# Another order for the last products, and other pieces of the last output rows

## The chip, the cores and the metric

The kernel runs on one core of one Trainium2 chip. A core has a matrix engine (TensorE, PE in the profile; its weight loads are PEld), a vector engine (VectorE, DVE), an activation engine (ScalarE, ACT), GpSimd (POOL), and SyncE (SP), which computes nothing and here issues DMAs. Sixteen DMA engines move data between the chip's memory (DRAM) and the core's on-chip memory; a DMA is issued from an engine's queue, here mostly SP's. Each engine runs its own list of instructions in order and waits on semaphores for the others. TensorE writes into PSUM, a small memory from which VectorE and ScalarE read.

The metric is the device time of one execution in microseconds (us); lower is better. Engine times within an execution come from a profile, which counts from the first instruction of the program to the last (the span).

## The reference

Attention with a block mask for 4 batches, 8 heads, 768 positions and 64 features a head; then a Fourier mixing over positions and features, a normalization, and two matrix products with a relu between them:

```python
attn = softmax(where(mask, scale * q @ k.T, -1e9)) @ v        # (4, 8, 768, 64)
x = attn.transpose(0, 2, 1, 3).reshape(4, 768, 512)
u = x + real(fft(fft(x, axis=1), axis=2))
un = (u - mean(u)) / sqrt(var(u) + 1e-6)
ch = maximum(un @ w_ch1, 0) @ w_ch2                           # 512 -> 2048 -> 512
return u + ch                                                 # (4, 768, 512) float32
```

## The kernel before

The work of a batch goes through attention, the Fourier stage, the normalization, the first product (`quad` in the kernel) and the second one. The program is one list of instructions in an order written out by hand: `slot` runs through the attention of all batches and puts pieces of the mixing of the batch before in between, by estimated times that `busy` adds up in `when`. After the last attention step only the last batch's mixing is left, and its pieces follow one another without anything between them. That last batch is done in another way than the first three (`last = b == B - 1`), and only it uses the functions `output_right`, `output_left` and `outputs`.

A batch's 768 rows stand in six tiles of 128 rows, three in `xA` (the first half, tiles 0 to 2) and three in `xB` (the second half, tiles 3 to 5). The Fourier stage wants rows s and -s together, so a tile's rows are not consecutive rows of the output. The table `_ORDER` says which they are: a tile is made of runs of rows, and `store` issues the DMAs for one tile: one for each run where the runs go backwards in the output, and one for a pair of runs where they go forwards. So tile 2 (`xA`, m = 2) leaves by two DMAs of 64 rows each, tile 5 (`xB`, m = 2) by one DMA whose rows are written as 2 x 64, and tile 4 (`xB`, m = 1) by one of 1 row, one of 2 x 63 rows, one of 1 row.

For the last batch the second product is done by Strassen's scheme in Winograd's form. The product has 2048 inner features; they are taken in two rounds (r = 0 and r = 1) of 1024. In a round, four `quad`s make the hidden features, then `outputs(r, m, after)` runs for m = 0, 1, 2. One call works on the pair of tiles m of `xA` and `xB` and splits each into its first 256 columns (a0 of `xA`, b0 of `xB`) and last 256 columns (a1, b1). Instead of eight block products it makes seven, named here by the order of Winograd's scheme: P1, P2, P3, P4 (right-hand sides 4), P5 (left sum 1), P6 (right-hand sides 2) and P7 (left sum 3). Each is four accumulating matmuls into one PSUM bank. VectorE then adds them into a0, a1, b0, b1 (`plus`), with a helper u that is P1 + P6 and later P1 + P6 + P7:

- a0 gets P1 + P2
- a1 gets P1 + P6 + P5 + P3
- b0 gets P1 + P6 + P7 + P4
- b1 gets P1 + P6 + P7 + P5

The left-hand sums of hidden features (`output_left(m, 1)` to `(m, 4)`) are VectorE work too. For m = 0 they are made inside the call; for the next tile they are made ahead, between this tile's sums (`ahead(j)`, which does nothing for the last m). The PSUM banks come from four pools: "m" and "s" of two banks, "t" and "o" of one. P1, P2, P3 use "m", P6 uses "t", P5 uses "o", P4 and P7 use "s". A bank can be written again once its reader has finished.

In the round r = 1 the finished rows are stored as each call goes on. In the last call (r = 1, m = 2, `ends` in the code) the second half's rows leave in three pieces: b1 once it is done, and b0, which is done last, in two DMAs of 128 columns, one from SP's queue and one from ScalarE's.

After the last store comes a branch: `with tc.If(over > 0): general()` (line 1574). `general` is a long slow path for inputs with very large scores; it is not taken here, but its code stands between the branch and the end of the program, and every engine has the branch in its list. Behind it each engine waits for what is outstanding, SP for the landing of all stores too, and a final barrier (line 1609) ends the program.

The lines that matter: 1115 to 1190 for the last batch's output stage, 1107 for the store, 1142 for the left-hand sums, 1159 for the matmuls of the seven products, 1166 for `plus`, 1175 for ScalarE's copy of P1, 1188 for the sum of u into both halves of `xB`, 1574 for the branch, 1609 for the end.

Of the kernel before, what the change touches and what calls it, by code (L numbers as in the profile page):

```python
# [82 lines left out]
def _rows(view, tile):  # L83

    got = []
    for t, p0, runs, jump, n, s0, step in _ORDER:
        if t != tile:
            continue
        at = view[s0:s0 + 1, :]
        row, col = list(at.ap[0])[0], list(at.ap[1])  # L90
        if jump > 0:
            got.append((p0, runs * n, bass.AP(tensor=at.tensor, offset=at.offset,
                                              ap=[[jump * row, runs], [step * row, n], col])))
            continue
        for r in range(runs):
            at = view[s0 + r * jump:s0 + r * jump + 1, :]
            got.append((p0 + r * n, n, bass.AP(tensor=at.tensor, offset=at.offset,
                                               ap=[[step * row, n], col])))
    return got
# [3 lines left out]
def kernel(  # L103
# [14 lines left out]
    nc = tc.nc  # L118

    B, H, S, D = q.shape  # L120
    DM = H * D
    FF = w_ch1.shape[1]
    P = 128
# [58 lines left out]
    ps_s = ctx.enter_context(tc.tile_pool(name="ps_s", bufs=2, space=PSUM))  # L182
    ps_o = ctx.enter_context(tc.tile_pool(name="ps_o", bufs=1, space=PSUM))
# [5 lines left out]
    when = {"PE": 0.0, "ACT": 0.0, "DVE": 0.0, "POOL": 0.0}  # L189
    free = {"m": [0.0, 0.0], "t": [0.0]}  # L190

    def busy(engine, us, after=0.0):
        when[engine] = max(when[engine], after) + us
        return when[engine]
# [283 lines left out]
    by_pe, to_gather = set(), deque()  # L478
    masks = {"by_pe": True}
# [68 lines left out]
    UP = 2 * C  # L548
    UNITS = len(pairs) * UP
    SLOT = 2  # L550
# [55 lines left out]
    def gather_to(u):  # L606
        while to_gather and to_gather[0] <= u:
            gather(to_gather.popleft())

    def gather(u):  # L610


        n, w = divmod(u, UP)
        half, c = divmod(w, C)
        if c == 0:
            return
        if c == 1:
            acc_of[n, half] = acc_p.tile([P, 2, HS], FP32, tag="acc", name="acc")
        acc, e = acc_of[n, half], e_of[u]
        start = e_of[u - 1] if c == 1 else acc  # L620
        at = max(e_at[u], acc_at.get((n, half), 0.0))
        if u in by_pe and masks["by_pe"] and w < UP - SLOT and max(when["DVE"], at) + 1.0 < max(when["POOL"], at) + 2.9:
            nc.vector.tensor_tensor(out=acc, in0=start, in1=e, op=ALU.add)
            acc_at[n, half] = busy("DVE", 1.0, at) + HOP
        else:

            for i in range(2):
                nc.gpsimd.tensor_add(out=acc[:, i, :], in0=start[:, i, :], in1=e[:, i, :])  # L628
            acc_at[n, half] = busy("POOL", 2.9, at) + HOP
        e_free[u] = acc_at[n, half]  # L630
# [320 lines left out]
    def mixer(b, xA, xB):  # L951
# [24 lines left out]
        t, s = {}, {}  # L976
# [127 lines left out]
        def store(half, m, cols=slice(0, DM), queue=nc.sync):  # L1104
            x = (xA, xB)[half]
            for p0, cnt, rows in _rows(out[b][:, cols], T * half + m):
                queue.dma_start(out=rows, in_=x[p0:p0 + cnt, m, cols])
            if m == T - 1:
                finished.add((b, half))
# [5 lines left out]
        o_t, o_s = {}, {}  # L1115
        DH = DM // 2

        def block(r, k, n):
            return w2_sb[:, 8 * r + 4 * k:8 * r + 4 * k + 4, n * DH:n * DH + DH]
# [10 lines left out]
        def output_left(m, j):  # L1130
            a11, a12, a21, a22 = (hs[g, i][:, :, m * P:(m + 1) * P]
                                  for i in range(2) for g in range(2))
            if j in (1, 3):
                o_s[m, j] = ep.tile([P, 4, P], FP32, tag="e", name="os")
            elif j == 4:
                o_s[m, j] = acc_p.tile([P, 4, P], FP32, tag="acc", name="os")

            to, a, c, op = {1: (o_s.get((m, 1)), a21, a22, ALU.add),
                            2: (a21, o_s[m, 1], a11, ALU.subtract),
                            3: (o_s.get((m, 3)), a22, a21, ALU.subtract),  # L1140
                            4: (o_s.get((m, 4)), a12, a21, ALU.subtract)}[j]
            tt(out=to, in0=a, in1=c, op=op)
            busy("DVE", 0.7)

        def outputs(r, m, after):

            if m == 0:
                output_left(m, 1)
                output_left(m, 2)
            a11, a12, a21, a22 = (hs[g, i][:, :, m * P:(m + 1) * P]  # L1150
                                  for i in range(2) for g in range(2))
            a0, a1 = xA[:, m, 0:DH], xA[:, m, DH:DM]
            b0, b1 = xB[:, m, 0:DH], xB[:, m, DH:DM]
            rights = {j: [o_t[j, 0], o_t[j, 1]] for j in (1, 2, 3, 4)}

            def product(pool, tag, a, c):
                ps = pool.tile([P, 512], FP32, tag=tag, name="yy")[:, 0:DH]
                for k in range(4):
                    nc.tensor.matmul(ps, a[:, k, :],  # L1159
                                     c[k // 2][:, k % 2, :] if isinstance(c, list) else c[:, k, :],  # L1160
                                     start=(k == 0), stop=(k == 3))
                busy("PE", 1.75)
                return ps

            def plus(to, a, c=None):
                tt(out=to, in0=a, in1=to if c is None else c, op=ALU.add)
                busy("DVE", 0.43)

            def ahead(j):
                if after is not None:  # L1170
                    output_left(after, j)

            u = sum_p.tile([P, DH], FP32, tag="oT", name="u")
            p1 = product(ps_m, "m", a11, block(r, 0, 0))
            nc.scalar.copy(out=u, in_=p1)
            plus(a0, p1)
            plus(a0, product(ps_m, "m", a12, block(r, 1, 0)))
            if m == 0:
                output_left(m, 3)
                output_left(m, 4)  # L1180
            plus(u, product(ps_t, "t", a21, rights[2]), u)
            plus(a1, u)
            p5 = product(ps_o, "o", o_s[m, 1], rights[1])
            plus(a1, p5)
            ahead(1)
            plus(u, product(ps_s, "s", o_s[m, 3], rights[3]), u)
            both = xB[:, m, :].rearrange("p (n d) -> p n d", n=2)
            tt(out=both, in0=both,
               in1=u.rearrange("p (o d) -> p o d", o=1).broadcast_to([P, 2, DH]), op=ALU.add)
            busy("DVE", 0.7)  # L1190
            plus(b1, p5)
            ends = r == 1 and after is None
            if ends:
                store(1, m, slice(DH, DM))
            ahead(2)
            p3 = product(ps_m, "m", o_s[m, 4], block(r, 1, 1))
            plus(a1, p3)
            if r == 1:
                store(0, m)
            ahead(3)  # L1200
            ahead(4)
            plus(b0, product(ps_s, "s", a22, rights[4]))
            if ends:
                store(1, m, slice(0, P))
                store(1, m, slice(P, DH), nc.scalar)
            elif r == 1:
                store(1, m)

        fl = [[("tm"[h == 1 and m != 1], lambda h=h, m=m: un_flip(h, m), 0.6, 0.55, 0.0)
               for m in range(T)]  # L1210
# [6 lines left out]
              for m, us in (((0, 2), RIGHT), ((1,), COMBINE))]  # L1217
        le = [("d", lambda i=i: left(0, i), 0.0, 0.0, COMBINE) for i in (1, 3, 4)]
        after = ([fl[0][0], sp[1][0]] + le +
                 [fl[0][2], sp[1][2], wh[1][0], fl[0][1], sp[1][1], wh[1][2],  # L1220
                  fl[1][0], fl[1][2], wh[1][1]] + ri[0] + [fl[1][1]] + ri[1])
        rest = []
        for r in range(2 if last else 0):
            rest += [(lambda p=p: quad(p), 7 * PRODUCT) for p in range(4 * r, 4 * r + 4)]
            rest += [(lambda r=r, m=m: outputs(r, m, m + 1 if m + 1 < T else None), 7 * 1.75)
                     for m in range(T)]
# [386 lines left out]
```

## Time and profile before

| what | value |
|---|---|
| median of 6 runs | 1064.7 us (1064.02 to 1069.03) |
| the profiled execution's own time | 1064.64 us |
| its span | 1062.9 us |
| mean granted TensorE clock | 0.997 |
| TensorE busy | 1036.2 us (97%) |
| the last batch's output stage, r = 0 | 942.5 to 979.1 us of the span |
| the same, r = 1 | 1015.2 to 1051.5 us |
| last sum on VectorE | 1051.54 to 1051.96 us |
| end of the span | 1062.9 us |

The span leaves out 1.7 us of the execution's own time. An idle engine costs nothing by itself; what counts is which engine, queue or transfer ended last, and in this program TensorE does until 1051.5 us. In the timeline, "x4" after a line is the number of instructions merged into it, and in square brackets stands how long the engine was idle before it and what released it.

### The profile page before, as it was taken

The page shows a single profiled execution, that of the slowest core. Times are in us where ns is not written, and L with a number is a line of the kernel's source. Part 1 is how long each engine was busy: PE and PEld are TensorE (multiplying, and loading weights), DVE is VectorE, ACT ScalarE, POOL GpSimd, SP SyncE. Part 2 cuts the span into 40 slices and gives each one's busy share as a digit, 9 for nine tenths or more (in the row PEclk, how much of TensorE's full clock was granted, in tenths as well). Part 3 has the DMA queues.
Part 4 walks back from the last instruction along what each step waited for, and adds up shares of the span by engine and source line. Part 5 has one row for each costly group of instructions (what it writes and reads, how often), then busy time and mean ns, then how long its engine had stood idle before and what let it go on. Part 6 is the DMA issues. An engine that isn't in the chain of part 4 may idle for free.

```text
span 1062.9 us, 12409 instructions
## 1 busy us (share of the span) xinstructions
PE 1036.2 (97%) x4390; PEld 536.2 (50%) x4390; DVE 654.0 (62%) x1218; ACT 374.1 (35%) x742; POOL 235.6 (22%) x262
## 2 busy tenths in 40 slices
PE   8999999999999999999999999999999999999995
PEld 4433345444455554444444555444445554578584
DVE  5899894667645445664578364765457355574663
ACT  6988855664030112342441302353221211210210
POOL 1000183537000002454553001256420001000000
PEclk9999999999999999999999999999999999999998
DMA  7757422220000002222230001221000001000001
GB/s 209 225 178 231 117 46 45 45 47 15 1 0 1 1 0 48 59 35 48 42 55 1 1 0 30 60 39 28 10 12 5 1 0 35 26 0 1 1 20 43
DMA packets 120741, 46.65 MB, mean 44 GB/s; under 512 B 108114, under 2 KB 113632, under 8 KB 120672
## 3 DMA queue, kind: packets, MB, share of 16 engines
q1 hardware_dynamic: 118654, 44.92, 17.1%
q10 hardware_dynamic: 1986, 0.85, 0.3%
q8 instruction: 36, 0.59, 0.2%
q14 instruction: 33, 0.27, 0.1%
q0 software_dynamic: 32, 0.01, 0.0%
HBM read 37.11 MB, written 6.29 MB: 41 GB/s over the span
## 4 chain that ended last, share of the span: by engine, by line
PE 87%; DVE 4%; ACT 3%; DMA 2%; issue 2%; SPq 1%; POOL 0%; ACTq 0%; POOLq 0%; DVEq 0%
PE y L1096 23%; PE z L1040 15%; PE s L569 11%; PE o L642 10%; PE yp L1040 7%; PE yy L1159 7%; PE xp L1040 4%; PE zp L850 2%; DMA out_dram<-x 1%; PE s L579 1%; PE zp L822 1%; PE sp L723 1%; PE utp L965 1%; ACT wraw L456 1%; ACT e L589 1%
## 5 line engine op out<-in xcount | busy, mean ns | idle before, releaser
L628 POOL TENSOR_TENSOR acc<-acc,e 128x384 f32<-128x384 f32 x158 | 159.3, 1044 | 94.1 <-DVE e L599 75.1
L569 PE MATMUL s<-qT,kT 64*128 64x384 f32 x768 | 153.2, 514 | 8.8 <-ACT e L589 5.3
L642 PE MATMUL o<-e,vr 128*64 128x384 f32 x768 | 141.7, 497 | 0.0
L1096 PE MATMUL y<-w_sb,hB 128*128 128x512 f32 x288 | 128.2, 596 | 1.0 <-DVE x L1099 1.0
L1096 PE MATMUL y<-w_sb,hA 128*128 128x512 f32 x288 | 128.4, 595 | 0.0
L599 DVE TENSOR_TENSOR e<-s,mask 128x768 f32<-128x768 f32 x92 | 83.8, 951 | 57.8 <-ACT s L597 48.0
L1099 DVE TENSOR_TENSOR x<-y,x 128x512 f32<-128x512 f32 x72 | 49.7, 690 | 110.9 <-PE y L1096 110.8
L569 PEld LDWEIGHTS s<-qT,kT 64*128 64x128 f32 x768 | 63.8, 185 | 87.1 <-issue 21.3
L597 ACT ACTIVATE s<-s 128x768 f32<-128x768 f32 x92 | 69.9, 792 | 87.6 <-PE s L569 87.0
L1040 PE MATMUL z<-unT,t 128*128 128x384 f32 x256 | 93.1, 486 | 1.2 <-DVE hA L1045 1.2
L628 POOL TENSOR_TENSOR acc<-e 128x384 f32<-128x384 f32 x42 | 47.1, 1142 | 212.3 <-ACT e L589 127.2
L1045 DVE TENSOR_TENSOR hA<-z,hA 128x384 f32<-128x384 f32 x64 | 35.7, 557 | 87.3 <-PE z L1040 87.3
L589 ACT ACTIVATE e<-s 128x768 f32<-128x768 f32 x100 | 76.1, 815 | 35.2 <-PE s L579 30.2
L1096 PEld LDWEIGHTS y<-w_sb,hB 128*128 128x128 f32 x288 | 53.4, 190 | 67.7 <-issue 64.8
L913 POOL TENSOR_SCALAR st<-st 128x1 f32<-128x1 f32 x24 | 8.6, 358 | 346.9 <-DVE st L912 346.9
L1096 PEld LDWEIGHTS y<-w_sb,hA 128*128 128x128 f32 x288 | 53.3, 190 | 62.8 <-issue 59.7
L642 PEld LDWEIGHTS o<-e,vr 128*64 128x64 f32 x768 | 47.9, 136 | 70.2 <-issue 68.3
L1049 ACT ACTIVATE hA<-hA 128x384 f32<-128x384 f32 x64 | 33.5, 523 | 120.3 <-DVE hA L1045 119.9
L1040 PEld LDWEIGHTS z<-unT,t 128*128 128x128 f32 x256 | 48.5, 190 | 35.5 <-DVE hA L1045 2.1
L1049 ACT ACTIVATE hB<-hB 128x384 f32<-128x384 f32 x64 | 33.5, 523 | 86.5 <-DVE hB L1045 84.2
L1060 ACT COPY hA<-xp 128x384 f32<-128x384 f32 x32 | 15.3, 478 | 97.9 <-PE xp L1040 97.9
L1040 PE MATMUL xp<-unT,w_sb 128*128 128x384 f32 x128 | 47.2, 492 | 0.0
(202 smaller groups left out, 1430.7 us busy)
## 6 DMA issues: line engine op xcount, KB each, us to landing
wraw<-in_moe_w_ch_dram SPq DMA_DIRECT2D x32, 512.0 KB
vr<-in_v_dram SPq DMA_DIRECT2D x30, 192.0 KB
qb<-in_q_dram SPq DMA_DIRECT2D x44, 96.0 KB
kb<-in_k_dram SPq DMA_DIRECT2D x44, 96.0 KB
x<-oT SPq DMA_DIRECT2D x192, 12.0 KB
out_dram<-x SPq DMA_DIRECT2D x17, 128.0 KB
out_dram<-x SPq DMA_DIRECT2D x7, 256.0 KB
qr<-in_q_dram SPq DMA_DIRECT2D x24, 64.0 KB
```

Of the source, the lines that this page charges most:

```text
L569: nc.tensor.matmul(s[:, i, 0:HS], kT[rows, c * P:(c + 1) * P], qT[rows, queries], start=True, stop=u not in by_pe)
L589: nc.scalar.activation(out=e, in_=s[:, :, 0:HS], func=ACT.Exp, scale=scale)
L597: nc.scalar.activation(out=s[:, :, 0:HS], in_=s[:, :, 0:HS], func=ACT.Exp, scale=scale)
L599: nc.vector.tensor_tensor(out=e, in0=s[:, :, 0:HS], in1=m.broadcast_to([P, 2, HS]), op=ALU.mult)
L628: nc.gpsimd.tensor_add(out=acc[:, i, :], in0=start[:, i, :], in1=e[:, i, :])
L642: nc.tensor.matmul(o[D * i:D * i + D, :], vt[:, i, c, :], e[:, i, :], start=(c == 0), stop=(c == C - 1))
L1040: nc.tensor.matmul(to, a[:, k, :], c[:, k, :], start=(k == 0), stop=(k == ND // 2 - 1))
L1045: tt(out=to, in0=ps, in1=a, op=ALU.add)
L1049: nc.scalar.activation(out=h, in_=h, func=ACT.Relu)
L1096: nc.tensor.matmul(y, hs[0, half][:, l, m * P:(m + 1) * P], w2_sb[:, 4 * r + l, :], start=(l == 0), stop=(l == 3))
L1099: nc.vector.tensor_tensor(out=x[:, m, :], in0=y, in1=x[:, m, :], op=ALU.add)
L1159: nc.tensor.matmul(ps, a[:, k, :], c[k // 2][:, k % 2, :] if isinstance(c, list) else c[:, k, :], start=(k == 0), stop=(k == 3))
```

## The change

In `outputs`, for every m and both rounds, P4 moves from the seventh place to the fourth, and P5 from the fourth to the sixth. The order P1, P2, P6, P5, P7, P3, P4 becomes P1, P2, P6, P4, P7, P5, P3. The sums move with them. The left-hand sums made ahead, which stood spread between the sums (1 after the sum of P5 into a1, 2 after the sums into `xB`, 3 and 4 after the sum of P3), now stand together: 1, 2 and 3 after the two sums of P5, ahead of the sum of P3, and 4 behind it.

In the round r = 1 the stores move as well. For m = 0 and 1 the second half's tile leaves after the sum of P5 into b1, the first half's after the sum of P3. For m = 2 the pieces are now: a0 after its second sum, b0 from ScalarE's queue after the sum of u into both halves, b1 after the sum of P5, and a1 at the end. Each is a half of the columns; the pieces of 128 columns are gone. The DMAs of that last call become 5 on SP's queue and 1 on ScalarE's, where there were 4 and 1.

In `gather` a comparison is given a name ahead of the `if` that uses it.

```diff
@@ gather
-        if u in by_pe and masks["by_pe"] and w < UP - SLOT and max(when["DVE"], at) + 1.0 < max(when["POOL"], at) + 2.9:
+        sooner = max(when["DVE"], at) + 1.0 < max(when["POOL"], at) + 2.9
+        if u in by_pe and masks["by_pe"] and w < UP - SLOT and sooner:
@@ outputs
+            ends = r == 1 and after is None
             u = sum_p.tile([P, DH], FP32, tag="oT", name="u")
             p1 = product(ps_m, "m", a11, block(r, 0, 0))
             nc.scalar.copy(out=u, in_=p1)
             plus(a0, p1)
             plus(a0, product(ps_m, "m", a12, block(r, 1, 0)))
+            if ends:
+                store(0, m, slice(0, DH))
             if m == 0:
                 output_left(m, 3)
                 output_left(m, 4)
             plus(u, product(ps_t, "t", a21, rights[2]), u)
             plus(a1, u)
-            p5 = product(ps_o, "o", o_s[m, 1], rights[1])
-            plus(a1, p5)
-            ahead(1)
+            plus(b0, product(ps_s, "s", a22, rights[4]))
             plus(u, product(ps_s, "s", o_s[m, 3], rights[3]), u)
             both = xB[:, m, :].rearrange("p (n d) -> p n d", n=2)
             tt(out=both, in0=both,
                in1=u.rearrange("p (o d) -> p o d", o=1).broadcast_to([P, 2, DH]), op=ALU.add)
             busy("DVE", 0.7)
+            if ends:
+                store(1, m, slice(0, DH), nc.scalar)
+            p5 = product(ps_o, "o", o_s[m, 1], rights[1])
             plus(b1, p5)
-            ends = r == 1 and after is None
-            if ends:
-                store(1, m, slice(DH, DM))
+            if r == 1:
+                store(1, m, slice(DH if ends else 0, DM))
+            plus(a1, p5)
+            ahead(1)
             ahead(2)
+            ahead(3)
             p3 = product(ps_m, "m", o_s[m, 4], block(r, 1, 1))
             plus(a1, p3)
             if r == 1:
-                store(0, m)
-            ahead(3)
+                store(0, m, slice(DH if ends else 0, DM))
             ahead(4)
-            plus(b0, product(ps_s, "s", a22, rights[4]))
-            if ends:
-                store(1, m, slice(0, P))
-                store(1, m, slice(P, DH), nc.scalar)
-            elif r == 1:
-                store(1, m)
```

## The prediction

> **What bounds the kernel now.** I read the chain that ended last first, then the stage that the diff touches, then what follows the last arithmetic. The chain in order of time ends so:
>
> ```profile
> 1015.24 36.27 PE yy L1159 x168
> 1051.51 0.02 issue
> 1051.54 0.42 DVE x L1166
> ```
>
> TensorE runs the 21 products of the last round without a gap: 36.27 / 21 = 1.727 us each. Then one sum, done at 1051.96. The span ends at 1062.9, so 10.9 us lie behind all arithmetic, and this chain does not explain them. Its waits do; from the branch's and the end's lines:
>
> ```profile
> L1574 PEldq COMPARE_BRANCH  x1: 3811/3811/3811, 1047.5 to 1047.5; - x1
> L1574 DVEq COMPARE_BRANCH  x1: 72/72/72, 1051.5 to 1051.5; - x1
> L1574 SPq COMPARE_BRANCH  x1: 50/50/50, 1052.6 to 1052.6; - x1
> L1574 ACTq COMPARE_BRANCH  x1: 62/62/62, 1053.4 to 1053.4; - x1
> L1574 DVEq EVENT_SEMAPHORE  x1: 21/21/21, 1056.1 to 1056.1; - x1
> ...
> L1574 ACTq EVENT_SEMAPHORE  x1: 17/17/17, 1060.9 to 1060.9; - x1
> ```
>
> Between its branch and its next instruction VectorE needs 4.5 us, though what that instruction waits for was over at 1052.0; TensorE's branch takes 3.8; ScalarE goes on 7.5 us after its branch, and SP's eight waits begin at 1060.9 too, 8.3 us after its own. From 1060.9 the closing waits and barrier take 2.0 us. So two things hold the end until 1060.9: stores that have not landed, and code that arrives late. The DMA view of the stretches behind (columns: stretch, its length, busy of PE, PEld, DVE, ACT, POOL, granted clock, DMA share, GB/s):
>
> ```profile
> 1027.60:1028.80 1.20, 1.20 (x7) 1.07 (x6) 0.39 (x2) 0.00 (x0) 0.00 (x0) 1.00 0.90 208
> 1041.70:1047.90 6.20, 6.20 (x31) 5.45 (x30) 2.00 (x5) 0.00 (x0) 0.00 (x0) 1.00 0.13 41
> 1050.90:1052.40 1.50, 0.60 (x3) 0.19 (x1) 0.42 (x1) 0.00 (x0) 0.00 (x0) 1.00 0.13 37
> ...
> 1055.90:1060.50 4.60, 0.00 (x0) 0.00 (x0) 0.00 (x0) 0.00 (x0) 0.00 (x0) 0.50 0.13 34
> ```
>
> The first is tile 0, two DMAs of 64 rows: 90% of the 16 DMA engines, 208 GB/s. The second is tile 4's 2 x 63 rows, the third b1's 2 x 64: share 0.13 is two engines of 16, at 37 to 41 GB/s. So `xB`'s tiles leave through two engines, `xA`'s through all. The last line is b0, issued at 1051.99 and moving only from 1055.9 to 1060.5, since its two engines still had b1 and their part of `xA`'s rows. In that stretch:
>
> ```profile
> q1 hardware_dynamic: 132, 0.07, 5.9%
> q10 hardware_dynamic: 130, 0.07, 4.9%
> q14 instruction: 3, 0.02, 1.9%
> ```
>
> SP's queue (q1) and ScalarE's (q10) move one piece of b0 each, and code (q14) comes in between.
>
> **The change part by part.** The sum is made against the profiled execution: 1064.64 us, span 1062.9, 1.74 around it; the median, 1064.7, stands 0.06 above it.
>
> *The comparison in `gather`, and the matmuls.* Same values, same matmuls: 0.
>
> *P4 fourth, P5 sixth.* P4 needs only hidden features and right-hand sides that were made in the quads. Each bank still has three or more products between uses, except P3's: it is last now, and the next tile's P2 takes its bank. The sum of P3 into a1 has the left-hand sums 1 to 3 ahead of it on VectorE. For m = 0, r = 1: P5 ends at 1015.24 + 6 x 1.727 = 1025.60; two sums start at 1025.63 and 1025.97 (neighbours start 0.34 apart now); left-hand sum 1 at 1026.31; 2 and 3, each waiting for the one before, 0.72 apart (0.68 long), at 1027.03 and 1027.75; the sum of P3 0.60 later, 1028.35 to 1028.77. The next P2 starts at 1027.33 + 1.73 = 1029.06, its first weight load 0.2 earlier: 0.1 to 0.3 us of room. Waiting behind that sum are left-hand sum 4 (until 1029.4) and a0's first sum, which follows ScalarE's copy at 1029.49 anyway. I take 0 for the four boundaries (two a round); bounds: 0, since TensorE has no gap to give back, and +0.8 (0.2 each, a load held until the sum ends).
>
> *Stores of m = 0 and 1.* `xB`'s tile leaves about 1.9 us earlier, `xA`'s about 2.3 later. The DMAs are the same and lie beside matmuls. What they can harm is the last tile: 2 x 63 rows took until 1048 on the two engines and end near 1046 now, before b0 asks for them. Below 0 is excluded, as nothing waits for them; above it by that slack. 0.
>
> *a0, two new issues on SP* at 1043.35 (P2 ends at 1042.88): 0.5 us of queue each, beside 8 us of matmul; nothing but b1's issue at 1050.3 is behind them. 0.
>
> *b0 earlier.* P7 ends at 1015.24 + 24.18 + 5 x 1.727 = 1048.06; its sum and the one into both halves end at 1049.23 (as now, 1048.54 + 0.69). ScalarE issues at 1049.25 and, at its 1.38 us, branches at 1050.65 instead of 1053.4. b1's issue at 1050.27 is 0.55 later than now.
>
> *The last issue.* P3 is done at 1051.51, the sum at 1051.96, as now. Then SP issues two DMAs instead of one, so it branches 0.57 later (0.52 long and a step), at 1053.16. ScalarE issues nothing there.
>
> *When the stores have landed.* b1 now moves 1.18 us after its issue (1049.72 to the 1050.9 of the third line). So b0 starts at 1050.45. b0 and b1 are 262 KB on two engines: at 51 GB/s (the steady part of tile 4's stretch, in finer slices) 5.1 us, at 37 GB/s 7.1 us, so until 1055.6 to 1057.5. Then a1's rows on these engines, 16 KB (0.4 us), and 0.4 us from the last packet (1060.5) to 1060.9: landed between 1056.4 and 1058.3 instead of 1060.9. All of b1 and most of b0 is moved while TensorE still works or in the 3 us after it.
>
> *When the code is there.* SP's own branch is the late one now. Bounds for what follows it: 3.8 us (TensorE's, few transfers beside it) and 8.3 (SP's now, which holds the landing too): 1057.0 to 1061.5. I take 5.0, near VectorE's 4.5, with 0.5 for a queue that is still busy around 1055: 1058.2. ScalarE, with 7.5 at the worst, is there at 1058.15.
>
> *The sum.* Both conditions met near 1058.3, less 2.6 from 1060.9. The closing 2.0 us stay. Span 1060.3, time 1060.3 + 1.74 = 1062.0.
>
> A rule that speaks against the change: the Trainium skill, "DMA: Bandwidth & Descriptors", in its section on where the fixed cost goes, fits a DMA as about 2.0 us plus bytes over 436 GB/s. By that the last store, issued at 1051.99, would have landed near 1054 now, and a second issue behind it would cost 0.57 us: 1065.2. The trace has 8.9 us for that store. The same page (section on why a DMA counts to 16) says that a DMA is spread over the largest number of engines up to 16 that divides its slowest dimension, lowest-numbered first, which is what the shares 0.90 and 0.13 show. "Runtime: NRT & Kernel Launch", on instruction fetch, says that a taken branch out of the loaded window fetches code by DMA before it goes on; the 4.5 us of VectorE agree.
>
> **The rivals.** Within 0.3% (3.2 us) of before is about what a measurement cannot tell from no change.
>
> *1. Code takes the place of the stores.* If ScalarE's and SP's 7.5 and 8.3 us are mostly code waiting behind whatever the two engines carry, SP's begins 0.57 later and lasts as long: ready at 1061.5, time 1065.2. For it: ScalarE owes nothing to a landing, yet goes on at 1060.9, when the stores end. Against: those engines empty some 3 us earlier then, and VectorE, branching in the same stretch, took 4.5.
>
> *2. The whole tail shrinks.* Code in 3.8 us, stores landed by 1057.0: span 1059.0, time 1060.7. For it: TensorE's branch. Against: b0 and b1 still lie on both engines when SP's code is asked for.
>
> *3. Slower: VectorE holds TensorE at the tile boundaries.* If P2's first matmul has to wait for the three left-hand sums put ahead of the sum of P3, 3 x 0.68 = 2.04 less the 0.27 of room is 1.8 us a boundary, 7.1 for four; less 2.6: 1069.1. It decides from (2.6 + 3.2) / 4 = 1.45 us a boundary. For it: room of 0.1 to 0.3. Against: the order above is worked from starts that the profile shows.
>
> **How the numbers follow.** Forecast 0.55, its own range 1061.0 to 1063.3; rival 1, 0.20; rival 2, 0.18; rival 3, 0.07. The likeliest gives 1062.0. Faster by over 0.3% is under 1061.5: rival 2 and about 0.12 of the forecast, 0.30. Slower by over 0.3% is rival 3, 0.07. The same holds 0.63. The range reaches to rival 2's side, 1060.2, and to most of rival 1, 1064.9, which leaves out its upper part and rival 3.
>
> **What would show it.** TensorE's last matmul at 1051.5 within 0.3 us and no gap over 0.2 at a tile's second product (else rival 3). ScalarE's branch near 1050.7, SP's near 1053.2. The last packets of q1 between 1056.2 and 1058, none of q10 after. SP's closing waits starting at 1057.5 to 1059. If q1 and q10 are empty by 1057 and SP's waits still begin at 1060.9 or later, rival 1 is right, and my prediction is wrong in its step on the code.

## The result, and the profile after

The changed kernel takes 1062.67 us (median of 19 runs, 1061.76 to 1063.69) where the kernel before takes 1064.83 (42 runs). The ratio is 0.9978, with a 95% interval of 0.9972 to 0.9984: 2.2 us, or 0.22%, less. That is under the 0.3% within which the prediction calls two kernels the same, but the interval lies clear of 1, so the kernel did become faster. The profiled execution took 1062.0 us, its span is 1060.3.

The chain of the changed kernel ends as it did before, with the 21 products of the last round:

```profile
1008.28 3.87 PE z L1041 x12
1014.73 36.36 PE yy L1160 x168
```

They take 36.36 us where they took 36.27, and this execution came to them 0.5 us earlier, in code that the change does not touch. So all times below are counted from the end of the last matmul, which is 1051.08 us of the span after and 1051.50 before. From there to the end of the span it was 11.43 us and is 9.21: the 2.2 us that the medians show lie there.

The branch's lines after (an engine's branch, and the first waits behind it):

```profile
L1576 SPq EVENT_SEMAPHORE  x8: 17/17/17, 1057.5 to 1058.6; - x8
...
L1576 ACTq COMPARE_BRANCH  x1: 62/62/62, 1050.0 to 1050.0; - x1
...
L1576 DVEq COMPARE_BRANCH  x1: 72/72/72, 1051.1 to 1051.1; - x1
L1576 SPq COMPARE_BRANCH  x1: 50/50/50, 1052.8 to 1052.8; - x1
L1576 DVEq EVENT_SEMAPHORE  x1: 21/21/21, 1054.0 to 1054.0; - x1
L1576 ACTq EVENT_SEMAPHORE  x1: 17/17/17, 1055.5 to 1055.5; - x1
```

ScalarE branches at 1050.0 and goes on at 1055.5, 5.5 us later, long before the end; VectorE needs 2.9 us. Neither is near the end any more. SP's first wait passes at 1057.46, and the trace has b1's landing at 1057.45; its second and third pass at 1057.89 and 1058.24, where the trace has the two pieces of a1 landing on the last DMA engine at 1057.87 and 1058.23. So SP had its code by then, and waited for rows.

What moved between (first the DMA queues from 1050.1 to 1053.9, then from 1053.9 to 1057.4; columns: packets, MB, share of 16 engines):

```profile
q10 hardware_dynamic: 129, 0.13, 12.4%
q1 hardware_dynamic: 16, 0.02, 3.8%
q8 instruction: 1, 0.02, 1.5%
q14 instruction: 1, 0.01, 0.7%
...
q1 hardware_dynamic: 274, 0.25, 24.9%
q14 instruction: 5, 0.04, 3.2%
q10 hardware_dynamic: 1, 0.00, 0.0%
```

In the first stretch nearly all is b0, from ScalarE's queue (q10): 0.13 MB, on the two DMA engines that 12.4% of sixteen are. b1 had been issued from SP at 1049.84, but no packet of SP's queue moves before 1053.3. In the second stretch come b1 and a1 (q1), and five code blocks between them.

### The profile page after: what moved, and what is told of

Same layout as the page of the kernel before. It is cut to its first block, busy times and chain, and to the rows that moved or that the text cites. A ratio compares the mean times of both kernels' runs of the same rounds, so it can differ in the third digit from the quotient of the medians.

```text
span 1060.3 us, 12418 instructions
## 1 busy us (share of the span) xinstructions
PE 1037.0 (98%) x4390; PEld 535.7 (51%) x4390; DVE 654.6 (62%) x1218; ACT 374.5 (35%) x742; POOL 235.7 (22%) x262
## 4 chain that ended last, share of the span: by engine, by line
PE 89%; DVE 3%; ACT 2%; DMA 2%; issue 1%; SPq 1%; POOL 0%; ACTq 0%; DVEq 0%
PE y L1097 23%; PE z L1041 15%; PE s L569 12%; PE o L643 11%; PE yp L1041 7%; PE yy L1160 7%; PE xp L1041 4%; PE zp L851 2%; PE s L579 1%; PE sp L710 1%; DMA out_dram<-x 1%; PE zp L823 1%; PE sp L724 1%; PE utp L966 1%; PE xt L666 1%
```

## The experiments

Theory 1, at the start: the second half's rows go through two DMA engines, which empty them one piece after the other, and the landing of the last of them holds the end. Theory 2: code that ScalarE and SP fetch behind the branch comes late and holds the end, and the change helps because ScalarE branches earlier.

All times below are medians, each beside runs of the kernel before on the same chip (1065.09 in the runs 1 to 4, 1064.3 in 5 to 8, 1064.43 in 9 to 12). The lines of the kernels differ by a few from those of the profile before.

### 1 and 2: no branch

```diff
-    with tc.If(over > 0):
-        general()
```

> The kernel before without the branch and the slow path behind it (the slow path, which these inputs never take, is left out). Theory 1, the last rows on two DMA engines hold the end: the stores stay where they are, only the code blocks no longer come between them, so the end of the span moves by at most 1.5 us, to 1063.3 or more of 1064.8. Theory 2, code that ScalarE and SP fetch late holds the end: 3.5 to 5 us faster, 1059.8 to 1061.3.

> The changed kernel without the branch and the slow path. Theory 1: the last landing (1058.2 of the span now) still holds the end, at most 1 us faster than the changed kernel, 1061.7 or more. Theory 2: its code is what is left, so it loses 2 us or more, to 1060.7 or less, and stands close to the kernel before without the branch.

The kernel before without the branch: 1063.62 us, ratio 0.9983 (0.9974 to 0.9992), 1.5 us faster. The changed kernel without it: 1060.92, ratio 0.9955 (0.9942 to 0.9969), 4.2 us faster than before and so about 1.8 faster than with the branch. Theory 2 wanted 3.5 to 5 us in the first, and the two kernels close together: they stand 2.7 us apart. The first fits theory 1 (1.5 us was its bound). The second lies between the two: theory 1 had allowed 1 us, theory 2 had asked for 2, and it gave 1.8 (its 1060.92 is 0.8 us below theory 1's bound and 0.2 above theory 2's).

The traces split what the branch costs. Counted from the last matmul, the last rows land at 8.39 us instead of 9.38 in the kernel before, at 5.87 instead of 7.15 in the changed one: 1.0 and 1.3 us of transfer. And from the last landing to the end of the span it is 1.4 and 1.25 us instead of 2.05; SP's eight waits behind the branch, which take about 0.6 us when nothing stops them, are gone. That second part I had not counted. So code does cost, but not by being late: its blocks get in the way of the rows. The trace names no DMA engine, but it shows this twice. In the kernel before, a code block moves from 1059.36 to 1059.66 and no row moves in that time, though 31 rows of b0 are still to come. And in the changed kernel the last piece of a1 lands on its two late engines at 5.95 and 7.15 us, without the branch at 5.85 and 5.87: with the code one of the two falls behind.

### 3: ScalarE's piece issued from SP

```diff
-                store(1, m, slice(P, DH), nc.scalar)
+                store(1, m, slice(P, DH))
```

> The kernel before, with the second 128-column piece of b0 issued from SP's queue too. ScalarE then branches some 10 us earlier and its code is there long before the stores have landed; the rows, their order and their two DMA engines are the same, SP branches 0.6 us later. Theory 1: 1064.8 within 0.6. Theory 2 (ScalarE's late code): 2 us or more faster, 1062.8 or less.

1063.82 us, ratio 0.9984 (0.9975 to 0.9993), 1.3 us faster. Neither: more than theory 1's 0.6, less than theory 2's 2. The branch's lines of this kernel:

```profile
L1574 SPq EVENT_SEMAPHORE  x8: 17/17/17, 1058.8 to 1060.6; - x8
...
L1574 ACTq COMPARE_BRANCH  x1: 54/54/54, 1041.5 to 1041.5; - x1
L1574 ACTq EVENT_SEMAPHORE  x1: 17/17/17, 1046.6 to 1046.6; - x1
...
L1574 SPq COMPARE_BRANCH  x1: 50/50/50, 1054.1 to 1054.1; - x1
```

ScalarE is through with its code at 1046.6, before the last tile's rows begin, and the end is still held: the last rows land 8.29 us behind the last matmul instead of 9.38, at 1060.2, and the rest of SP's waits pass behind that. The gain is 1.1 us of landing, nearly the same as without the branch. Theory 2 as stated falls here. What stays of it becomes part of theory 1: code blocks that are fetched while the last rows move delay them, by about 1 us in all. This run also puts both pieces of b0 into one queue; that this is not what helped follows from runs 2 and 10 (below).

### 4 and 9: the second half's rows later

The fourth run stored b0 (ScalarE) and b1 (SP) behind a1; the ninth issued both from SP:

```diff
-            if ends:
-                store(1, m, slice(0, DH), nc.scalar)
...
-            if r == 1:
-                store(1, m, slice(DH if ends else 0, DM))
+            if r == 1 and not ends:
+                store(1, m)
...
                 store(0, m, slice(DH if ends else 0, DM))
+            if ends:
+                store(1, m, slice(0, DH), nc.scalar)        # run 9: without nc.scalar
+                store(1, m, slice(DH, DM))
```

> The changed kernel, with b0 and b1 of the last call stored behind a1, at the end. Products, sums, pieces and queues are the same; only the time at which the two engines' rows leave is moved, b0 by 2.7 us, b1 by 2.2. Theory 1: the landing moves by as much, 1064.5 to 1065.5, the gain is gone. If the order of the products is what brings the gain: 1062.7 within 0.5.

> The changed kernel, with b0 and b1 of the last call both issued from SP, behind a1. In the run before this one only b1 was late: ScalarE's queue waits for nothing but b0's own sum, so it had issued b0 when it always does. Now b0 leaves 4.0 us later than in the changed kernel, b1 3.6. Theory 1 (two DMA engines empty the second half's rows one piece after the other, and that holds the end): they start 2.9 us after the last matmul and need 6 to 6.5 us, the end moves by 2 to 3 us, 1064.4 to 1065.7. If the order of the products or the cut into halves is what brings the gain: 1062.7 within 0.5.

Run 4: 1062.34 us, ratio 0.9971 (0.996 to 0.9982), as fast as the changed kernel. The expectation was wrong, since its premise was: ScalarE's queue waits for nothing but b0's sum, so b0 was issued 2.23 us ahead of the last matmul's end, exactly as in the changed kernel, and only b1 was late, by 3 us. That this cost nothing is a finding of its own: in the changed kernel b1's first row moves 2.3 us behind the last matmul, when b0 is nearly through (its last rows end at 2.5 and 2.8), so b1 gains nothing by being issued sooner.

Run 9 does what run 4 was meant to do, with the order of products, the halves and all sums as in the changed kernel: 1064.8 us, ratio 1.0001 (0.9992 to 1.001). The whole gain is gone. Its lines:

```profile
L1577 SPq EVENT_SEMAPHORE  x8: 17/17/17, 1057.5 to 1061.3; - x8
...
L1577 ACTq EVENT_SEMAPHORE  x1: 17/17/17, 1046.8 to 1046.8; - x1
...
L1577 DVEq EVENT_SEMAPHORE  x1: 21/21/21, 1054.4 to 1054.4; - x1
L1577 SPq COMPARE_BRANCH  x1: 50/50/50, 1054.5 to 1054.5; - x1
```

SP's waits begin 3.0 us after its branch, so its code is early, and they last until 1061.3: b1 lands at 1061.0, 9.65 us behind the last matmul. Its closest neighbour is run 10 (below), which also issues everything from SP and differs only in the place of the two stores: there b0 leaves 4.2 us sooner and b1 3.8, the last landing is 3.8 us sooner, and the median, 1061.33, is 3.5 us lower. The order of the products is worth nothing by itself; it is worth what it does for the time at which the second half's rows leave.

### 5 and 11: whole tiles, and pieces without the new order

```diff
 # run 5, on the changed kernel
-            ends = r == 1 and after is None
+            ends = False
 # run 11, on the kernel before
+            if ends:                      # behind the second sum of a0
+                store(0, m, slice(0, DH))
...
-                store(0, m)
+                store(0, m, slice(DH if ends else 0, DM))
...
-                store(1, m, slice(0, P))
-                store(1, m, slice(P, DH), nc.scalar)
+                store(1, m, slice(0, DH), nc.scalar)
```

> The changed kernel, with the last call's tiles stored whole like the others: xB's after the sum of P5, xA's after the sum of P3 (no halves, no issue on ScalarE). Theory 1: the two engines start on 262 KB 1 us later than they do now, and carry 8 rows of 2 KB of xA behind it instead of 1 KB: landing 1 to 1.7 us later, 1063.7 to 1064.4. If the halves are worth nothing: 1062.7 within 0.3.

> The kernel before with its own order of products, but the new pieces: a0 leaves after its second sum, b1 after the sum of P5, a1 after the sum of P3, b0 last as one piece from ScalarE. Theory 1: b0 still comes last on the two engines, which only have 4 rows of 2 KB less to move in front of it: 0.3 to 1 us faster than before, 1063.6 to 1064.3 where before is 1064.6. If the cut into halves is the gain: 1062.5.

Run 5, the new order with whole tiles: 1062.65 us, ratio 0.9983 (0.9974 to 0.9992). The last landing is at 7.50 us behind the last matmul, 0.35 later than in the changed kernel, not the 1 to 1.7 of the expectation. But this run changes two things, for without b0's own issue ScalarE is out of the tail: it branches at 1042.2. The run that shares this and keeps the halves is again run 10, and beside it whole tiles land 1.7 us later (7.50 and 5.82), as expected, with ratios 1.3 us apart (0.9983 and 0.9971). So the halves do seem to be worth something, and what ScalarE's code costs hides it in the comparison with the changed kernel. The intervals of these two ratios overlap a little, so by the times alone it is not shown.

Run 11, the pieces with the old order: 1063.03 us, ratio 0.9986 (0.9977 to 0.9995), 1.4 us faster, more than the 0.3 to 1 expected. a0 leaves early, b0 leaves in one piece of 1 KB rows, and the last landing is at 7.92 us instead of 9.38. So the pieces alone bring more than half of what the whole change brings. The gains of the parts do not simply add up, since all of them relieve the same two engines, and what the new order brings with ScalarE left in the tail and whole tiles was not run.

### 6: no b0 at all

```diff
             if ends:
-                store(1, m, slice(0, P))
-                store(1, m, slice(P, DH), nc.scalar)
+                finished.add((b, 1))
```

> The kernel before without the store of b0 (those rows' first columns are left out of the output). It measures what the last store costs by itself. Theory 1: the end falls to the landing of xA's rows (1057.2 of the span) or SP's code, 3 to 4 us faster, 1060.8 to 1061.8. Theory 2: SP and ScalarE branch 0.6 and 10 us earlier, and SP's code still takes 8 us: 1064.2.

1059.54 us, ratio 0.995 (0.9937 to 0.9964), 4.8 us faster than before. That is the price of the kernel before's last store, and more than expected; it includes what ScalarE's code costs, since without an issue of its own ScalarE branches at 1042.4. The lines show what is left without it:

```profile
L1573 SPq EVENT_SEMAPHORE  x8: 17/17/17, 1056.9 to 1057.4; - x8
...
L1573 DVEq COMPARE_BRANCH  x1: 72/72/72, 1052.7 to 1052.7; - x1
L1573 SPq COMPARE_BRANCH  x1: 50/50/50, 1052.8 to 1052.8; - x1
L1573 DVEq EVENT_SEMAPHORE  x1: 21/21/21, 1057.2 to 1057.2; - x1
```

SP's eight waits all pass within 0.5 us, and begin 4.1 us after its branch; the last rows had landed 0.2 us before that. VectorE needs 4.5 us. So here the rows are no longer what SP waits for; what comes last is most likely its code, 4.1 us behind the branch in this run.

### 7, 8, 10 and 12: what the theory says would be better

Run 7 moves P2 of the last call behind P5, so that b0 and b1 are done one product earlier. Run 8 issues b1 from GpSimd's queue. Run 10 issues b0 from SP's queue. Run 12 is run 7 with b0 from SP's queue.

```diff
 # runs 7 and 12, on the changed kernel
-            plus(a0, product(ps_m, "m", a12, block(r, 1, 0)))
-            if ends:
-                store(0, m, slice(0, DH))
+            if not ends:
+                plus(a0, product(ps_m, "m", a12, block(r, 1, 0)))
...
             ahead(3)
+            if ends:
+                plus(a0, product(ps_m, "m", a12, block(r, 1, 0)))
+                store(0, m, slice(0, DH))
 # runs 10 and 12
-                store(1, m, slice(0, DH), nc.scalar)
+                store(1, m, slice(0, DH))
 # run 8: store(1, m, ..., nc.gpsimd) for b1
```

> The changed kernel, with P2 moved behind P5 in the last call alone: P1, P6, P4, P7, P5, P2, P3. b0 and b1 are done and leave one product (1.73 us) earlier, a0 two products later. Theory 1: the two engines are empty 1.7 us earlier, and a1's part follows without a wait; the end falls by 1 to 1.7 us to 1061.0 to 1061.7, unless SP's code now comes last. Theory 2: SP's branch is where it was, 1062.7 within 0.3.

> The changed kernel, with b1 issued from GpSimd's queue instead of SP's. If its rows go to other DMA engines than b0's, theory 1 says that the two queues empty side by side and the end falls by 1 to 2 us, 1060.7 to 1061.7; if they go to the same two engines, 1062.7 within 0.5. GpSimd's own work for the DMA can cost as much as is gained, since it starts only after b1's sum.

> The changed kernel, with b0 issued from SP's queue in the same place. The rows leave when they do now; ScalarE has nothing at the end and branches 8 us earlier, so its code blocks come before the rows. Theory 1: the two engines lose no time to ScalarE's code, 0 to 1 us faster, 1061.7 to 1062.7. If ScalarE's issue beside SP's is worth something: slower than 1062.7 by 0.3 or more.

> The version with P2 behind P5 in the last call (second half's sums first), with b0 issued from SP's queue, so that ScalarE's code is loaded long before the end. Theory 1: the end falls by 0 to 1 us below that version's 1060.8, to 1059.8 to 1060.8; the bound below is SP's code, 4.1 us after its branch in the run without b0, which gives 1060.0.

| run | median, us | ratio to before | last landing | end of the span |
|---|---|---|---|---|
| before | 1064.83 | 1 | 9.38 | 11.43 |
| changed | 1062.67 | 0.9978 (0.9972 to 0.9984) | 7.15 | 9.21 |
| 7 | 1060.83 | 0.9966 (0.9954 to 0.9978) | 6.05 | 7.93 |
| 8 | 1062.62 | 0.9981 (0.9972 to 0.999) | 7.19 | 9.02 |
| 10 | 1061.33 | 0.9971 (0.996 to 0.9981) | 5.82 | 7.88 |
| 12 | 1059.67 | 0.9956 (0.9942 to 0.9969) | 4.46 | 6.43 |

(Landing and end in us behind the last matmul, from one profiled execution each.) Run 10's profiled execution took 1063.75 us, 2.4 above that run's median, but it lost this ahead of its last matmul. Run 7 was faster than expected by 0.2 us, run 10 by 0.4, run 12 by 0.1; the kernel before was 0.4 to 0.5 us faster beside these runs too, so they came out about as expected. Taken one by one, 7 and 10 touch or overlap the changed kernel's interval; run 12 does not, and is the fastest version here: 4.8 us under the kernel before and, by the two ratios, some 2.3 under the changed one.

Run 10 and run 2 belong together. With b0 on SP's queue and ScalarE's code out of the way the last landing is at 5.82; with b0 on ScalarE's queue and no code at all it is at 5.87. So the queue by itself costs nothing, and the 1.3 us to the changed kernel's 7.15 are put down to ScalarE's code (each landing is from one execution). From run 7 to run 12 the same move is worth 1.6 us of landing. The lines of run 10:

```profile
L1576 SPq EVENT_SEMAPHORE  x8: 17/17/17, 1059.6 to 1060.3; - x8
...
L1576 ACTq EVENT_SEMAPHORE  x1: 17/17/17, 1049.7 to 1049.7; - x1
...
L1576 SPq COMPARE_BRANCH  x1: 50/50/50, 1056.4 to 1056.4; - x1
```

Run 8 brought nothing. GpSimd needed 0.95 us to issue the DMA, its rows began only 2.4 us behind the last matmul, when b0 was nearly through, and b1 was now the last to land, at 7.19, where from SP's queue it had landed at 6.37 with a1 behind it. The trace does not name the DMA engines, but the rows of b1 move at most two packets at a time, and two of the sixteen shares of a1 land late (5.8 to 6.8 us, the others by 4.5) as they do in the changed kernel; so b1 again went through two engines only, and through two that a1 needs as well.

In run 12 the waits behind the branch look like those without b0:

```profile
L1578 SPq EVENT_SEMAPHORE  x8: 17/17/17, 1055.1 to 1055.7; - x8
...
L1578 ACTq EVENT_SEMAPHORE  x1: 17/17/17, 1046.3 to 1046.3; - x1
...
L1578 SPq COMPARE_BRANCH  x1: 50/50/50, 1052.4 to 1052.4; - x1
L1578 DVEq EVENT_SEMAPHORE  x1: 21/21/21, 1054.7 to 1054.7; - x1
```

SP's waits begin 2.7 us after its branch and pass without a stop: nothing is left that waits for rows alone. The bound of 1060.0 in the expectation, worked from the 4.1 us of run 6, did not hold: how long the code takes differs from run to run.

### The runs together

From the last landing to the end of the span it is 1.7 to 2.1 us in every run that has the branch and all stores, from the fastest (4.46 and 6.43) to the slowest (9.65 and 11.51), and the medians follow. In the run without b0, where code most likely comes last, it is 2.25. This is what shows theory 1: as long as SP's code is there first, the last landing sets the end, and it moves with the time at which the two engines get their rows and with what else they carry, the code among it.

## Why the prediction was right

The forecast was 1062.0, the result 1062.67; the size was 2.7 us forecast, 2.2 measured. By its steps:

- *P4 fourth, P5 sixth: 0, bounds 0 and +0.8.* The weight load of the next tile's P2 did wait for the sum of P3: 0.18 us at each of two boundaries in the last round, and 0.7 us of VectorE waits in all for the four. TensorE's stage became 0.09 us longer, 36.36 for 36.27; the first round 0.08. So the term is +0.2. Rival 3 is excluded by these numbers. The lines for one boundary:

```profile
1027.85 0.42 DVE L1167 TENSOR_TENSOR x<-yy,x 128x256 f32<-128x256 f32 x1
1028.18 0.68 DVE L1143 TENSOR_TENSOR os<-hA,hB 128x512 f32<-128x512 f32 x1
1028.32 1.59 PEld L1160 LDWEIGHTS yy<-w_sb,hA 128*128 128x128 f32 x8 [0.18 <-DVE x L1167]
```

  The sum of P3 ends at 1028.27, and the weight load starts behind it. On the clock of the profile before that is 1028.78, as forecast (1028.77); but the load was due before it, so the 0.1 to 0.3 us of room were not there, and it was the bound that covered the loss.
- *Stores of m = 0 and 1, and a0: 0.* No later piece waited for them. Right.
- *b0 earlier.* Forecast 2.26 us ahead of the last matmul's end, measured 2.23; ScalarE's branch 0.86 ahead, measured 1.08 (its issue took 1.13 us, not 1.38). Right.
- *The last issue.* SP's branch 1.65 us behind the last matmul, measured 1.72. Right. a1's second issue took 0.65 us.
- *Landing between 1056.4 and 1058.3.* On the same clock, 4.9 to 6.8 us behind the last matmul; measured 7.15. This is the term that was mis-sized, by 0.4 us beyond its upper end: of what the two engines lose to code blocks I had counted nothing, and runs 1 to 3 put that at 1.0 to 1.3 us. The prediction also had all of b1 and most of b0 moved within 3 us of the last matmul. It was the other way round: b0 was through by then and b1 had only begun, since b1 waits for b0. That changes nothing in the sum, which takes both together.
- *Code, 1058.2.* This step named the wrong cause for the same moment. Behind its branch SP had its code no later than 4.7 us (the first wait ends with a landing, so it may have been sooner), 3.0 us in run 9 and 2.7 in run 12. ScalarE took 5.5, less than the 7.5 that I had carried over; why is not shown. Rival 1, in which SP's 8.3 us stay, is excluded by these 4.7 us, and for ScalarE's part by run 3, where ScalarE's code was loaded by 1046.6 and 1.1 us was all that came of it.
- *The closing 2.0 us.* Last landing 7.15, end 9.21: 2.06. Right.

So the mechanism, rows on two DMA engines, was right and is shown by run 9 beside run 10, and the saving was 0.5 us too large. That the span came out at the forecast 1060.3 is partly luck: the tail was 0.4 us longer than forecast, and that execution was 0.4 us ahead before it began. It is luck too that the step on the code, whose cause was wrong, gave 1058.2, near the upper end of the landing's range: the middle of that range, about 1057.3, would have put the forecast 1 us lower. Which DMA engines carry a piece no trace here records; the shares 0.90 and 0.13 say how many, and that pieces wait for one another says that `xB`'s pieces share theirs.

The rule of a fixed 2.0 us plus bytes over 436 GB/s, which would have made the change worth nothing or a loss, comes from the Trainium skill, "DMA: Bandwidth & Descriptors", section "Anatomy of one DMA — SWDGE (gpsimd) path", where it is fitted to DMAs issued from GpSimd. It does not hold for the last stores of this tail, which SP and ScalarE issue: the last store took 8.9 us from issue to landing before the change, and still 3.5 in run 12.

## What to carry to other kernels

Look at how each of the last stores is spread over the DMA engines, not at how many bytes it has: a piece whose rows form two runs went through two engines of sixteen at 37 to 51 GB/s, and should be computed and issued first, so that pieces that spread over all engines come last (run 7). Where a branch follows, take every engine but the one that must issue the last store out of the tail: here ScalarE's code, fetched while the last rows moved, delayed them by 1.1 to 1.6 us (runs 3, 10 and 12). And measure the tail from the end of the last matmul to the last landing: here that is where nearly all of the difference between the versions lay, while the chain of work stops at the last sum.

## What was unexpected of the hardware

- One queue's piece was emptied before another's began on the same two engines: b1, issued 1.24 us ahead of the last matmul's end, moved its first packet 2.3 us behind it, when b0 was nearly through; delaying its issue by 3 us cost nothing (run 4).
- Issuing a DMA does not always take the same time: the second piece of a1 (of the whole `xA` tile in run 5) took 0.65 us on SP in the changed kernel, 1.21 in run 10 and 1.75 in run 5, where the first took 0.48 to 0.52. What held it the traces do not show.
- The same branch cost an engine between 2.7 us (SP, run 12) and 8.3 (SP, before), as long as the wait for rows is counted with it, and 2.9 to 4.6 for VectorE, which waits for no rows.
